# First two batches of a windowed attention: plain head pairs loaded in 1.5 KB runs and turned by fp32 products with the identity

## The chip, the cores and the metric

The kernel runs on one core of a Trainium2 chip. The metric is the device time of one execution in microseconds, the median of the runs of a kernel. The core has a matrix engine (TensorE, in the profile PE, its weight loads PEld), a vector engine (VectorE, DVE), a scalar engine (ScalarE, ACT), GpSimd (POOL), and SyncE (SP), which here issues all DMAs.

## The reference

Three layers follow each other; all inputs are float32.

```python
batch, n_heads, seq, head_dim = (4, 8, 576, 64)
scores = scale * np.matmul(q, k.transpose(0, 1, 3, 2))
mask_plain = (rel >= 0) & (rel < 32)
mask_dil = (rel >= 0) & (rel < 128) & (rel % 4 == 0)
masks = np.stack([mask_plain if h < H // 2 else mask_dil for h in range(H)], axis=0)
...                                     # softmax over the masked scores
x = (attn @ v), as [2304, 512]
h = x @ w_in                            # 512 -> 2048
x2 = (h - np.tanh(h)) @ w_out           # 2048 -> 512
...                                     # soft mixture of 8 experts of 4 slots each over x2
```

So each query of heads 0 to 3 (the plain heads) sees itself and the 31 keys before it, and each query of heads 4 to 7 (dilated) every fourth of the 128 last ones.

## The kernel before

Heads are taken in pairs: pairs 0 and 1 are plain, 2 and 3 dilated. For each of four batches the order is `PO = (2, 3, 0, 1)`. Batches 0 and 1 are laid out by a list of steps with due times (`at(t, f, ...)` and the loop that sorts them, from L778 on): scores, norms, transposes and values of batch 0, then of batch 1, between them the conversion of w_out and w_in and the first 512 tokens of the x @ w_in layer. Batches 2 and 3 run inside the loop over the hidden layer of batches 1 and 2 (class `Attn`), where TensorE multiplies without a break. The order of each engine's queue is the order in which the program is written.

The pieces that the change and the prediction speak of:

- `load_qk` (L206) brings q and k of one head pair into a tile `rqk` of 96 partitions. A partition x holds the rows 6x to 6x+5 of both heads. For plain pairs L214 interleaves the heads (row, head, 64 numbers), one DMA for each head and each of q and k, 256 bytes at a time. For dilated pairs L219 takes 3 KB runs, one DMA each for q and k. SP issues all of them in the order of the program and can wait only in that order.
- `emit_qk` (L247) turns one of q or k so that the head's 64 numbers lie in partitions: six TensorE transposes (L267) of 96 x 128 for a head pair, three into each of two PSUM tiles, each then copied out by ScalarE or VectorE (L97 for k, L275 or L277 for q, which is scaled on the way). The upper 64 partitions hold the second head.
- `emit_scores` (L283): mask product L291, scores L305 (for plain pairs 12 products of 64 x 64 weights and 96 moving columns, head 0 in the array's upper, head 1 in its lower rows), largest value L314 on VectorE, exponentials L317 on ScalarE.
- `emit_norm` (L323): 1/sum on VectorE (L326, L328), the product L329 on GpSimd. `emit_trans` (L332): transposes of the probabilities L338 on TensorE. `emit_pv` (L343): products with v, L359, one head into the lower, one into the upper half of the output's partitions.
- The w_out weights come as 64-bit numbers (`load_w`, L409) in tiles of 1 MB for two steps each; a step's conversion starts on GpSimd (L430), goes on on VectorE (L441 to L446) and feeds TensorE's transposes L468 and the products L479 and L492. Its float32 form is written back to HBM (L475).
- `emit_h` (L498): the products of the hidden layer, L503 to L505.

In the order by due time the loads of batch 0 stand among the w_out tiles: SP issues w_out steps 0 and 1 (4.53 us), v and then q and k of the first plain pair, w_out steps 2 and 3 (13.10 us), v of that pair, w_out steps 4 and 5, a write of w_out, q and k of the second plain pair, and so on.

Of the kernel before, what the change touches and what calls it, by code (L numbers as in the profile page):

```python
# [59 lines left out]
def moe_kernel(ctx: ExitStack, tc: tile.TileContext, q, k, v, w_in, w_out, phi, w1, w2, out):  # L60
    nc = tc.nc
# [4 lines left out]
    NP = H // 2  # L66
# [11 lines left out]
    def mm(shape):  # L78
        return ps_m.tile(shape, F32, tag="mm", name="mm")
# [15 lines left out]
    def copy(eng, out, in_):  # L95

        (nc.scalar.copy if eng == "A" else nc.vector.tensor_copy)(out=out, in_=in_)  # L97
# [7 lines left out]
    def unit(name, shape, dt=F32):  # L105
        return sb.tile(shape, dt, tag="unit", bufs=UNITS, name=name)

    def cpart(*dims):
        o = moff[0]
        moff[0] += size(dims)  # L110
        return view(mem[:, o:o + size(dims)], dims)
# [35 lines left out]
    ident = cpart(128)  # L147
# [55 lines left out]
    raws, vt, qT, kT = {}, {}, {}, {}  # L203
    sc_p, sc_s, sc_pt, qks = {}, {}, {}, []

    def load_qk(b, p):  # L206


        t = unit("rqk", [96, 2, 12 * D])
        for n, src in enumerate((k, q)):  # L210
            src = src[b, 2 * p:2 * p + 2]
            if p < NP // 2:
                for hh in range(2):
                    nc.sync.dma_start(  # L214
                        out=t[:, n].rearrange("x (a h d) -> x a h d", a=6, h=2)[:, :, hh, :],
                        in_=src[hh].rearrange("(x a) d -> x a d", a=6),
                    )
            else:
                nc.sync.dma_start(out=t[:, n], in_=src.rearrange("h (x a) d -> (h x) (a d)", a=12))  # L219
        raws[b, p] = t  # L220
# [26 lines left out]
    def emit_qk(b, p, n):  # L247

        if n == 0:
            if not qks:  # L250
                t = sb.tile([128, 2, 2 * S], F32, tag="qk", name="qk")
                qks.append(Ring([t[:, 0], t[:, 1]]))

            qT[b, p] = qks[0].next()
            kT[b, p] = qT[b, p][:, S:2 * S]
        raw = raws[b, p][:, n].rearrange("x (j c) -> x j c", j=6)
        t = qT[b, p][:, 0:S] if n else kT[b, p]
        if p < NP // 2:

            t = t.rearrange("p (x e r) -> p e r x", e=2, r=3)  # L260
        else:

            t = t.rearrange("p (h r x e) -> p r e h x", h=2, r=2, e=3)
        for th in range(2):
            ps = mm([128, 3, 96])
            for r in range(3):
                nc.tensor.transpose(ps[:, r, :], raw[:, 3 * th + r if p < NP // 2 else 2 * r + th], ident[0:96, 0:96])  # L267
            dst = t[:, th]
            if p >= NP // 2:
                ps = ps.rearrange("p e (h x) -> p e h x", h=2)  # L270
            eng = ENGS["qk"][4 * min(b, 2) + 2 * n + th]
            if n == 0:
                copy(eng, dst, ps)
            elif eng == "A":
                nc.scalar.activation(out=dst, in_=ps, func=ACTF.Copy, scale=0.125)  # L275
            else:
                nc.vector.tensor_scalar(out=dst, in0=ps, scalar1=0.125, scalar2=None, op0=ALU.mult)  # L277
# [439 lines left out]
    class Attn:  # L717
# [5 lines left out]
        def load(self, nqk, nv):  # L723
            while self.nqk < min(nqk, NP) or self.nv < min(nv, NP):
                if self.nqk < min(nqk, NP):
                    load_qk(self.b, PO[self.nqk])
                    self.nqk += 1
                if self.nv < min(nv, NP):
                    load_v(self.b, PO[self.nv], nc.sync)
                    self.nv += 1  # L730

        def turn(self, s):

            for p, n in ([(s, 0), (s, 1)] if s < 3 else [(3, s - 3)] if s < 5 else []):
                emit_qk(self.b, PO[p], n)
                if n:
                    self.load(p + 3, p + 2)
            if 0 < s <= NU // 2:
                for i in (2 * s - 2, 2 * s - 1):
                    emit_trans(self.b, i)  # L740
# [32 lines left out]
    with tc.manual_schedule():  # L773
# [7 lines left out]
        for b, (t0, dt) in enumerate((ATT0, ATT1)):  # L781
            for i in range(NU):
                t = t0 + dt * i
                at(t, emit_scores, b, i)
                at(t + NORM[b] * dt, emit_norm, b, i)
                at(t + TRANS[b] * dt, emit_trans, b, i)
                at(t + PV[b] * dt, emit_pv, b, i)
                if b == 0 and i < NWARM:
                    at(t + WAT * dt, warm, WARM)
            for p in range(NP):  # L790
                for n in range(2):
                    at(t0 - 0.02 + 0.01 * n if p == 0 else t0 + dt * (3 * p - 3 + n + QK[b]), emit_qk, b, PO[p], n)
                at(t0 + dt * 3 * p - LQK[b], load_qk, b, PO[p])
                at(t0 + dt * 3 * p - LV[b], load_v, b, PO[p], nc.sync)
        at(DT0 + ATT0[1] * 5, consts2)
        for p in range(2):
            at(ATT1[0] + ATT1[1] * (12 + 3 * p) - LQK[1], load_qk, 2, PO[p])
        at(ATT1[0] + ATT1[1] * 12 - LV[1], load_v, 2, PO[0], nc.sync)
        at(TPHI, lambda: nc.sync.dma_start(out=phi_sb, in_=phi.rearrange("(k p) s -> p k s", p=128)))
        for e in range(NFT):  # L800
            t, dt = (WO1[0] + WO1[1] * e, WO1[1]) if e < KA else (WO2[0] + WO2[1] * (e - KA), WO2[1])
# [6 lines left out]
            t, dt = WI[0] + WI[1] * e, WI[1]  # L808
# [11 lines left out]
        for ft in range(NFT):  # L820
            t = HT[0] + HT[1] * ft
# [23 lines left out]
        for ch in range(1, 4):  # L845
            xh, xl = xhi[ch], xlo[ch]
            if ch == 3:
# [6 lines left out]
                t = unit("gr", [128, 3, 512])  # L854
# [4 lines left out]
            for s in range(NFT // 2):  # L859
                a, b = 2 * s, 2 * s + 1  # L860
# [40 lines left out]
        for s in range(NFT // 2):  # L901
            a = 2 * s
            ps = ps_h.tile([128, 512], F32, tag="h", name="h").rearrange("p (i t) -> p i t", i=2)
# [57 lines left out]
        for a, copy in enumerate((nc.scalar.copy, nc.vector.tensor_copy)):  # L961
            ps = mm([128, 2, 128])
# [7 lines left out]
        ps = mm([128, 512])  # L970
        for c in range(4):
            for fq in range(4):
                nc.tensor.matmul(
                    ps[32 * fq:32 * fq + 32, :], lhsT=tT[:, c, 32 * fq:32 * fq + 32], rhs=wo[fq][:, c, :],
                    start=(c == 0), stop=(c == 3), tile_position=(0, 32 * fq),
# [7 lines left out]
        for a, copy in enumerate((nc.scalar.copy, nc.vector.tensor_copy)):  # L983
            ps = mm([128, 2, 32])
# [32 lines left out]
        for cols in halves:  # L1017
            ps = mm([96, 256])
# [3 lines left out]
                out=sS[64:96, cols], in0=ps[64:96], in1=sS[64:96, cols].bitcast(F32), op=ALU.subtract  # L1022
# [49 lines left out]
```

## Time and profile before

| | |
|---|---|
| median of 3 runs | 500.41 us (499.46 to 501.45) |
| the profiled execution | 501.07 us, its span 499.3 us |
| mean granted TensorE clock in it | 0.96 of full speed |
| busy in the span: PE, PEld | 470.8 us (94%), 351.4 us (70%) |
| DVE, ACT, POOL | 222.9, 236.0, 83.6 us |
| DMA packets | 60740, of them under 512 bytes 35600 |

The profile comes from one execution. It is read by stretch: TensorE is the busy engine nearly all the time, but not from the start. For the first 80 us the attention of batch 0, the conversion of the weights and the loads run against each other, and the granted clock of TensorE changes between its full and its half speed; later TensorE hardly pauses. A busy time of TensorE says that matmuls were under way, not how full the array was: matmuls overlap, and their time from start to end is longer than the time until the next one starts.

### The profile page before, as it was taken

To read this page: it belongs to the slowest core of one execution; us is meant where nothing else is said; L and a number is where in the kernel's file an instruction comes from. 1 tells how busy PE (TensorE), PEld (TensorE's weight loads), DVE (VectorE), ACT (ScalarE), POOL (GpSimd) and SP (SyncE) were. 2 spreads that over 40 slices of the span, in tenths; PEclk is the share of its full clock that TensorE was granted. 3 is DMA by queue.
4 is the path that set the end of the run, shared out by engine and by line. 5 is a ranking of instruction groups with operands and counts; after the bars stand their busy time and mean duration, and the time that the engine had idled before them with its cause. 6 is when DMAs were issued, how large, how long until landed. Compare 5 with 4: busy or idle time off the path is not lost.

```text
span 499.3 us, 11253 instructions
## 1 busy us (share of the span) xinstructions
PE 470.8 (94%) x4531; PEld 351.4 (70%) x4531; DVE 222.9 (45%) x558; ACT 236.0 (47%) x763; POOL 83.6 (17%) x99
## 2 busy tenths in 40 slices
PE   6989888999999999999999899999999999999981
PEld 4767676877777867888787678877678869845430
DVE  1787888954754445543252454332221223232132
ACT  3857536575655464665365356543132323313121
POOL 3463444432341010111011011100000000010000
PEclk9967768999999999999999999999999999999996
DMA  9997799444145401222320100209600259899938
GB/s 247 277 262 258 258 336 269 151 117 121 35 139 123 96 3 39 76 59 49 81 44 1 37 1 2 86 4 390 254 29 0 85 180 402 304 389 410 409 146 334
DMA packets 60740, 81.14 MB, mean 163 GB/s; under 512 B 35600, under 2 KB 39440, under 8 KB 60688
## 3 DMA queue, kind: packets, MB, share of 16 engines
q1 hardware_dynamic: 60688, 80.42, 49.7%
q8 instruction: 36, 0.59, 0.5%
q14 instruction: 16, 0.13, 0.1%
HBM read 71.50 MB, written 8.91 MB: 161 GB/s over the span
## 4 chain that ended last, share of the span: by engine, by line
PE 85%; DVE 6%; ACT 4%; issue 1%; DMA 1%; POOL 0%; POOLq 0%; ACTq 0%; DVEq 0%
PE h L503 14%; PE h L505 13%; PE h L504 13%; PE mm L305 6%; PE mm L537 5%; PE lg L518 4%; PE mm L359 4%; PE mm L338 4%; PE mm L635 3%; PE mm L267 3%; PE h L686 3%; PE y L711 3%; ACT mem L317 2%; PE warm L200 1%; PE mm L468 1%; PE mm L479 1%
## 5 line engine op out<-in xcount | busy, mean ns | idle before, releaser
L503 PE MATMUL h<-xhi,whi 128*128 128x512 f32 x256 | 107.1, 418 | 0.0
L505 PE MATMUL h<-xhi,wlo 128*128 128x512 f32 x256 | 101.0, 395 | 0.0
L504 PE MATMUL h<-xlo,whi 128*128 128x512 f32 x256 | 100.8, 394 | 0.0
L509 ACT ACTIVATE mem<-h 128x512 f32<-128x512 f32 x56 | 33.4, 596 | 83.7 <-PE h L505 83.7
L512 DVE TENSOR_TENSOR mem<-h,mem 128x512 f32<-128x512 f32 x56 | 38.6, 689 | 73.6 <-ACT mem L509 73.4
L329 POOL TENSOR_TENSOR mem<-mem 128x320 f32<-128x320 f32 (+1 forms) x48 | 34.5, 718 | 195.7 <-DVE mem L328 132.7
L503 PEld LDWEIGHTS h<-xhi,whi 128*128 128x128 f32 x256 | 48.8, 191 | 13.3 <-issue 5.0
L505 PEld LDWEIGHTS h<-xhi,wlo 128*128 128x128 f32 x256 | 48.5, 189 | 10.9
L504 PEld LDWEIGHTS h<-xlo,whi 128*128 128x128 f32 x256 | 48.9, 191 | 8.4
L97 ACT COPY g<-mm 128x512 f32<-128x512 f32 x72 | 40.2, 596 | 12.0 <-PE mm L550 4.8
L317 ACT ACTIVATE mem<-mm,mem 128x80 f32<-128x80 f32 (+1 forms) x84 | 26.8, 330 | 30.1 <-DVE mem L314 30.1
L305 PE MATMUL mm<-qk 64*64 64x96 f32 (+2 forms) x672 | 36.0, 254 | 2.1 <-DVE qk L97 2.0
L317 ACT ACTIVATE mem<-mem 128x80 f32<-128x80 f32 (+1 forms) x84 | 29.9, 357 | 16.5 <-DVE mem L314 14.5
L305 PEld LDWEIGHTS mm<-qk 64*64 64x64 f32 (+1 forms) x672 | 29.0, 139 | 10.6 <-issue 5.6
L97 ACT COPY mem<-mm 80x448 f32<-80x448 f32 (+4 forms) x64 | 26.7, 442 | 10.1 <-DVE xlo L391 6.5
L338 PE MATMUL mm<-mem 112*80 112x112 f32 (+1 forms) x168 | 25.4, 279 | 5.0 <-POOL mem L329 2.8
L311 DVE TENSOR_TENSOR mem<-mm,mem 128x320 f32<-128x320 f32 (+1 forms) x24 | 11.3, 470 | 41.8 <-PE mm L305 41.8
L512 DVE TENSOR_TENSOR gr<-h,gr 128x512 f32<-128x512 f32 x16 | 11.1, 691 | 42.2 <-ACT gr L509 42.2
L359 PEld LDWEIGHTS mm<-mem,v 80*64 80x64 f32 (+1 forms) x672 | 23.8, 144 | 7.8 <-issue 4.2
L359 PE MATMUL mm<-mem,v 80*64 80x48 f32 (+1 forms) x672 | 28.6, 234 | 0.0
L267 PE MATMUL mm<-mem,rqk 96*128 96x96 f32 x192 | 23.2, 262 | 5.1 <-DMA rqk<-in_k_dram 4.1
L460 POOL TENSOR_TENSOR wlo<-cvb,whi 128x512 fp32r<-128x512 f32 x16 | 21.5, 1343 | 38.0 <-DVE whi L97 14.4
(153 smaller groups left out, 749.3 us busy)
## 6 DMA issues: line engine op xcount, KB each, us to landing
ex<-in_moe_w_dram SPq DMA_DIRECT2D x30, 1024.0 KB, 10.6
raww<-in_moe_w_out_dram SPq DMA_DIRECT2D x8, 1024.0 KB, 8.7
raww<-in_moe_w_in_dram SPq DMA_DIRECT2D x8, 1024.0 KB, 5.9
wo_dram<-cva SPq DMA_DIRECT2D x16, 256.0 KB, 5.1
wo<-wo_dram SPq DMA_DIRECT2D x4, 1024.0 KB, 5.8
out_dram<-o SPq DMA_DIRECT2D x8, 512.0 KB, 4.8
v<-in_v_dram SPq DMA_DIRECT2D x24, 160.0 KB, 3.9
v<-in_v_dram SPq DMA_DIRECT2D x16, 192.0 KB, 3.4
```

Source lines behind the costliest of these rows:

```text
L97: (nc.scalar.copy if eng == "A" else nc.vector.tensor_copy)(out=out, in_=in_)
L267: nc.tensor.transpose(ps[:, r, :], raw[:, 3 * th + r if p < NP // 2 else 2 * r + th], ident[0:96, 0:96])
L305: nc.tensor.matmul(ps[64 * x:64 * x + nr, c, :], lhsT=qT[b, p][r, q0:q0 + nr], rhs=kT[b, p][r, k0:k0 + nk], start=not by_pe, stop=True, sk ...
L317: nc.scalar.activation(out=pr[:, c, :], in_=ps[:, c, :], func=ACTF.Exp, bias=nm[:, c:c + 1], accum_out=sm[:, c:c + 1],)
L329: nc.gpsimd.tensor_tensor(out=pr, in0=pr, in1=rc.unsqueeze(2).to_broadcast([128, nb, nk]), op=ALU.mult)
L338: nc.tensor.transpose(ps[:, c, :], pr[0:P, c, :], ident[0:P, 0:P])
L359: nc.tensor.matmul(o[64 * hh:64 * hh + 64, col:col + nq], lhsT=vt[b, p](n, hh), rhs=pt[:, c, 64 * x:64 * x + nq], start=True, stop=True,)
L503: nc.tensor.matmul(ps, lhsT=wh, rhs=xh[:, kt, :], start=(kt == 0), stop=False)
L504: nc.tensor.matmul(ps, lhsT=wh, rhs=xl[:, kt, :], start=False, stop=False)
L505: nc.tensor.matmul(ps, lhsT=wl, rhs=xh[:, kt, :], start=False, stop=(kt == KT - 1))
L509: nc.scalar.activation(out=g, in_=ps, func=ACTF.Tanh)
L512: nc.vector.tensor_tensor(out=g, in0=ps, in1=g, op=ALU.subtract)
```

## The change

For plain pairs of batches 0 and 1, `load_qk` issues one DMA for k and one for q instead of two each. Both heads' rows go one head behind the other into the partition, 6 rows x 64 numbers = 1.5 KB in one run. A transpose of 128 columns that are two heads' 64 can't be taken from that layout with one step, so `emit_qk` takes, for each of the six rows, two ordinary fp32 products: the head's 96 x 64 piece is the weight, the identity the moving operand (96 columns), and the result goes to the lower or the upper 64 partitions of the PSUM tile. What lies in PSUM, and all that follows, is the same. Batches 2 and 3 and the dilated pairs stay as they were.

```diff
--- before.py
+++ after.py
@@ -209,12 +209,16 @@
         t = unit("rqk", [96, 2, 12 * D])
         for n, src in enumerate((k, q)):
             src = src[b, 2 * p:2 * p + 2]
-            if p < NP // 2:
+            if p < NP // 2 and b >= 2:
                 for hh in range(2):
                     nc.sync.dma_start(
                         out=t[:, n].rearrange("x (a h d) -> x a h d", a=6, h=2)[:, :, hh, :],
                         in_=src[hh].rearrange("(x a) d -> x a d", a=6),
                     )
+            elif p < NP // 2:
+                nc.sync.dma_start(
+                    out=t[:, n].rearrange("x (h c) -> x h c", h=2), in_=src.rearrange("h (x a) d -> x h (a d)", a=6)
+                )
             else:
                 nc.sync.dma_start(out=t[:, n], in_=src.rearrange("h (x a) d -> (h x) (a d)", a=12))
         raws[b, p] = t
@@ -264,6 +268,14 @@
         for th in range(2):
             ps = mm([128, 3, 96])
             for r in range(3):
+                if p < NP // 2 and b < 2:
+
+                    for hh in range(2):
+                        nc.tensor.matmul(
+                            ps[64 * hh:64 * hh + 64, r, :], lhsT=raws[b, p][:, n, 64 * (6 * hh + 3 * th + r):][:, 0:64],
+                            rhs=ident[0:96, 0:96], start=True, stop=True,
+                        )
+                    continue
                 nc.tensor.transpose(ps[:, r, :], raw[:, 3 * th + r if p < NP // 2 else 2 * r + th], ident[0:96, 0:96])
             dst = t[:, th]
             if p >= NP // 2:
```

## Rows read from the trace of the kernel before

**Rows 1.** The page's granted TensorE clock, tenths of full speed, 40 slices of 12.5 us.
```profile
PEclk9967768999999999999999999999999999999996
```
**Rows 2.** By stretch: length, busy us of each engine (instructions), granted clock, DMA share, GB/s.
```profile
core 0: us, PE busy (x) PEld busy (x) DVE busy (x) ACT busy (x) POOL busy (x), PEclk, DMA share, GB/s
...
25.64:29.06 3.42, 2.10 (x36) 1.60 (x34) 2.00 (x7) 2.48 (x13) 3.20 (x6) 1.00 0.93 172
29.06:42.71 13.65, 13.59 (x120) 9.86 (x120) 10.71 (x25) 7.55 (x23) 6.42 (x8) 0.50 0.97 308
...
56.37:70.02 13.65, 11.49 (x69) 9.06 (x70) 11.47 (x25) 5.00 (x14) 7.69 (x6) 0.50 0.96 278
...
73.43:76.84 3.41, 1.64 (x17) 1.31 (x15) 3.35 (x5) 2.79 (x6) 2.91 (x2) 1.00 1.04 361
76.84:80.26 3.42, 3.23 (x37) 2.65 (x38) 1.96 (x5) 1.36 (x9) 0.00 (x0) 0.50 1.07 305
80.26:489.80 409.54, 402.14 (x3837) 299.11 (x3836) 167.45 (x432) 190.10 (x599) 47.37 (x52) 1.00 0.41 137
288.47:291.88 3.41, 2.66 (x25) 2.25 (x24) 2.39 (x10) 2.21 (x7) 0.72 (x1) 1.00 0.00 0
```
**Rows 3.** Waits, 22 to 31 us: total us, times, longest.
```profile
POOL cva L430 <- DMA raww<-in_moe_w_out_dram: 3.0, 1, 3.0
...
PE mm L338 <- POOL mem L329: 1.8, 2, 1.4
```
**Rows 4.** GpSimd in order of time: start us, us, operation, [idle before <-releaser].
```profile
22.08 1.05 POOL L430 TENSOR_TENSOR cva<-raww,mem 128x512 f32<-128x512 f32 x1 [3.03 <-DMA raww<-in_moe_w_out_dram]
...
27.34 1.04 POOL L430 TENSOR_TENSOR cva<-raww,mem 128x512 f32<-128x512 f32 x1
28.34 0.72 POOL L329 TENSOR_TENSOR mem<-mem 128x320 f32<-128x320 f32 x1
```
**Rows 5.** TensorE in order of time, around 29 us.
```profile
29.12 0.97 PE L338 MATMUL mm<-mem 112*80 112x112 f32 x4 [1.38 <-POOL mem L329]
...
30.36 1.22 PE L305 MATMUL mm<-qk 64*64 64x96 f32 x12
```
**Rows 6.** SP's issues in order of time: start us, us, line, xcount.
```profile
7.17 1.95 SPq L214 DMA_DIRECT2D rqk<-in_k_dram  x2
9.44 3.62 SPq L214 DMA_DIRECT2D rqk<-in_q_dram  x2
13.10 1.24 SPq L409 DMA_DIRECT2D raww<-in_moe_w_out_dram  x1
```
**Rows 7.** DMA packets from 12.4 to 14.4, 14.4 to 17.5 and 69.4 to 71 us.
```profile
DMA packets 1100, 0.43 MB, mean 213 GB/s; under 512 B 895, under 2 KB 1100, under 8 KB 1100
...
DMA packets 1590, 0.73 MB, mean 237 GB/s; under 512 B 1505, under 2 KB 1505, under 8 KB 1589
...
DMA packets 324, 0.63 MB, mean 396 GB/s; under 512 B 19, under 2 KB 19, under 8 KB 324
```
**Rows 8.** Tile rqk, 7 to 13 us: time from issue to landing.
```profile
DMA to landing us min/median/max: 7.3/7.4/8.1
```
**Rows 9.** ScalarE in order of time, around 29 us.
```profile
28.35 1.25 ACT L275 ACTIVATE qk<-mm 128x288 f32<-128x288 f32 x2
```
**Rows 10.** The chain that ended last, in order of time: start us, us, what.
```profile
38.10 1.15 PE mm L267 x6
...
41.10 1.15 PE mm L305 x12
...
46.11 0.64 PE mm L305 x12
...
47.11 0.50 PE mm L359 x12
...
112.39 0.50 PE mm L267 x6
```
**Rows 11.** TensorE by line and form, 288.47 to 291.88 us: busy us, mean ns.
```profile
L338 PE MATMUL mm<-mem 112*80 112x112 f32 x8 | 1.1, 261 | 0.7 <-ACT g L97 0.7
L537 PE MATMUL mm<-mem 128*128 128x128 f32 x8 | 1.0, 272 | 0.0
```

## The prediction

> **What bounds the kernel now.** I read the granted clock and the engines' shares by stretch first, because the edit lies in the first quarter of the span only. From 80 us on TensorE is busy 402.1 of 409.5 us at full clock [rows 2]: there nothing is gained except by giving TensorE less to do, and what was gained before 80 us arrives at the end unchanged. Before 80 us it is otherwise. TensorE's clock stands at its lower level (1.2 instead of 2.4 GHz) for three stretches, 29.06 to 42.71, 56.37 to 70.02 and 76.84 to 80.26 [rows 2]; they are the dips in the page's clock line [rows 1]. Before the first fall the engine was busy only 2.10 of 3.42 us, before the third 1.64 of 3.41 [rows 2]. In the low stretch that starts at 29.06 TensorE works almost without a pause (13.59 of 13.65 us), VectorE for 10.71 [rows 2].
>
> So I asked what makes the pause before 29.06. The waits from 22 to 31 us name it: GpSimd waits 3.0 us for a w_out tile to land, and TensorE 1.8 us, in two waits, for GpSimd [rows 3]. On GpSimd, in order: the conversion at L430 starts at 22.08, when its tile has landed; then come a normalisation, a mask, the next L430 at 27.34 and the normalisation L329 at 28.34 [rows 4]. TensorE's transposes L338 wait 1.38 us for that one and start at 29.12; the scores L305 follow at 30.36 [rows 5]. GpSimd is busy 3.20 of the 3.42 us up to 29.06 [rows 2], so a tile that lands sooner moves this whole string. SP had issued the first plain pair's loads just ahead of that tile: four pieces from 7.17 on, the tile at 13.10 [rows 6].
>
> **The change, part by part.**
>
> *Loads.* For pairs 0 and 1 of batches 0 and 1, four DMAs of 256-byte runs (4 x 576) become two of 1.5 KB runs (2 x 192); the bytes stay at 4 x 144 KB = 0.59 MB. From 12.4 to 14.4 us, where 895 of 1100 packets are under 512 bytes, the DMA engines move 213 GB/s, from 14.4 to 17.5, where 1505 of 1590 are, 237; from 69.4 to 71 us, where nearly all are larger than 2 KB, 396 [rows 7]. The old load thus takes 0.59/213 = 2.8 us of full DMA time. No row has 1.5 KB runs by themselves. If they go no faster than the small ones, nothing is gained (0); if as fast as the large ones, 0.59/396 = 1.5 us, a gain of 1.3. In size 1.5 KB is nearer to the large ones, so I take 1.0 us (0 to 1.3) for all that is queued behind the first load.
>
> The Trainium skill, DMA: Bandwidth & Descriptors, Specifications, gives 512 bytes as the least transfer for full rate. By that rule 1.5 KB runs go at the large ones' rate and the gain is the upper bound, 1.3 us. The trace agrees as far as its 213 against 396 GB/s reach, but other sizes are mixed in.
>
> *SP.* Two issues fewer per pair. The old ones took 1.95 us for two and 3.62 for two [rows 6], the last of them held back, and landed 7.3 to 8.1 us after issue [rows 8]. SP is free earlier, but the DMA engines behind it are full at that time, so I count nothing beside the 1.0 us. Were they not full, the tile could start up to 13.10 - 9.44 = 3.7 us sooner; I keep that for the clock rival. The second load stands ahead of weights that GpSimd takes after they have landed, and the two of batch 1 land long before their transposes after 100 us: 0, hidden under TensorE's unbroken work. Without that cover they would be worth up to 1.3 us each.
>
> *From the tile to TensorE.* 1.0 us earlier at L430, which waited 3.03 [rows 4], moves L329 and L338 by 1.0, L338 to 28.1. What is late next is ScalarE: the scores at 30.36 need its copies of q, L275, two from 28.35 lasting 1.25 us, so until 29.60 [rows 9]. The scores then gain at most 30.36 - 29.60 = 0.76. I take 0.75 (0 if the tile comes no earlier; 1.3 if ScalarE moves too). It is a lead in low-clock work, worth half once the clock is up again at 42.71: **-0.4 us** (0 to -0.7).
>
> *TensorE.* 48 transposes (8 groups of 6, 96 moving columns) become 96 products (8 groups of 12, two heads side by side in the array's columns). No row has that form; two are near. The scores L305, 12 fp32 products of 96 moving columns in pairs that share the array by rows, take 0.64 us at full clock and 1.15 at the low one; the values L359, 12 products that share it by columns as the new ones do, but with 64 moving columns, 0.50 [rows 10]. An old group of 6 takes 0.50 at full clock and 1.15 at the low one [rows 10]. If the pairs overlap, a new group is 0.50 to 0.64; if they don't, 12 x (0.50/6 = 0.083) = 1.0. I take 0.64, the row with the same moving width: L359 at 0.50/12 = 0.042 each is half of a transpose, so column pairs do overlap. At the low clock that is 1.15 for 1.15. At 112.39, between full-array work, 0.50 becomes 0.64; the changes of tiling beside it may cost as much again: +0.2. Of the other seven four follow L359 and two precede it, in the same tiling; a change of tiling saved is worth at most 0.14 (the same 0.64 - 0.50), and half of it on three groups that nothing hides is -0.2. Those before 27 us lie beside GpSimd's string and count nothing; uncovered they are 0.14 each, either way. Copies out of PSUM stay. **0.0 us** (-0.4 to +0.5).
>
> *Sum.* **-0.4 us.** The profiled execution is 501.07 us, 1.8 of it around its span of 499.3, and lies 0.7 above the median of 500.41. That makes the span 498.9, such an execution 500.7, and the median **500.0**.
>
> **The rivals.**
>
> *The clock doesn't fall at 29.06.* The pause before it shrinks from 1.38 us to what ScalarE still causes, and L338 moves ahead of 29.06. A stretch busy 2.66 of 3.41 us (288.47 to 291.88) kept the full clock, one busy 2.10 of 3.42 lost it [rows 2]; with the pause down to some 0.8 us the stretch before 29.06 would be busy about 2.6 of 3.42. Then 13.6 us of TensorE's work no longer takes twice its time, but VectorE, busy 10.71 of those 13.65, lets at most 2.9 be gained: I take 2.4, and with the 0.4 it is **497.6** (-2 to -4, where the tile comes sooner still). Against it: VectorE then sets the pace, TensorE pauses again, and the fall may only come later.
>
> The Trainium skill, TensorE: Matmul & The Clock Gate, Part 4, says that transposes don't count as activity for the clock as other products do. By that, 12 transposes turned into 24 products before 27 us would by themselves make this rival likelier. The trace speaks against the rule: from 288.47 to 291.88 at least 16 of the 25 TensorE instructions were transposes [rows 11] and the clock stayed at 1.00 [rows 2]. So this case's chance rests on the pause alone.
>
> *A fall that lasts longer: slower than before.* The third low stretch lasted 3.42 us, the two before it 13.65 [rows 2]. It follows a pause in which VectorE keeps TensorE waiting (1.64 of 3.41 busy). If the work arrives so shifted that this fall lasts as long as the others, 10.2 us more, of a stretch in which TensorE hardly rests, run at half speed: +5.1, less 0.4, **505.1**. It decides once TensorE's work after 76.84 is thinner than its 3.23 of 3.42 us now. For it: nothing pins the pauses. Against it: the shift that I expect is below 1 us.
>
> *Column pairs don't overlap.* 1.0 instead of 0.64 a group, six groups that nothing hides, one of them at half clock: 7 x 0.36 = +2.5, less 0.4: **502.5**. L359 speaks against it.
>
> *The loads move nothing.* The tile is held by something else, or another wait ends at the same time: **500.4**.
>
> **How the numbers follow.** Forecast 0.46; clock stays up 0.32; longer fall 0.08; no overlap 0.04; nothing moves 0.10. About 0.5%, 2.5 us, is what a measurement of this kernel can tell from no change. Faster than 497.9: most of the second case, 0.26. Slower than 502.9: the longer fall, part of no overlap, some other fall of the clock, 0.11. The rest, 0.63, is the same. The range takes in the clock case down to -3.9, and upwards loads without gain, the dearer TensorE groups and 1 us of scatter (the runs before reach 1.0 above their median): 496.5 to 501.9. It leaves out the longer fall, no overlap and the clock case's tail, under 2 in 10. The likeliest case's own range is 499.2 to 501.0.
>
> **What would show it.** L430 at 21.1 instead of 22.08, its wait 2.0; L338 near 28.1; L305 near 29.6; groups of 12 at 0.64 in the chain; 4 x (2304 - 384) = 7680 fewer packets. The clock line tells the rivals apart: the dips in their places (forecast), the first gone or later (clock case), the last longer (slower). I am wrong if L430 starts no earlier, or if a group takes 1.0 us.

## The result, and the profile after

The change makes the kernel slower by 0.3 to 0.9 per cent in the median; the first and the third interval lie above 1, the second just takes in 1. Three sets of runs of the changed kernel, each beside runs of the kernel before on the same chip, gave

| | changed | before | ratio [95%] |
|---|---|---|---|
| first set | 504.06 us (501.54 to 506.74, 8 runs) | 500.29 us (8 runs) | 1.0085 [1.0061, 1.0109] |
| second set | 502.16 us (498.01 to 504.37, 12 runs) | 499.72 us (34 runs) | 1.0027 [0.9996, 1.0058] |
| third set | 503.67 us (500.03 to 506.73, 12 runs) | 499.70 us (17 runs) | 1.0076 [1.0045, 1.0106] |

The forecast was 500.0 us with a range up to 501.9; the first and the third median lie above it by about 2 us, the second by 0.3. The profiled execution of the first set took 502.19 us, with a span of 500.4 (before: 501.07 and 499.3). It is the second fastest of its eight runs, and its span is only 1.1 us longer, where the medians are 3.8 apart.

The page's clock line of the changed kernel answers to [rows 1]. The dip that stood in the third and fourth slices (near 29 us) is gone; a new one stands in slice 23, near 280 us.

```profile
PEclk9999878999999999999999899999999999999996
```

The stretches of the changed kernel, in the columns of [rows 2]: first the two that held the pause and the low clock before, then the two at the new dip.

```profile
25.64:29.06 3.42, 2.49 (x52) 1.99 (x44) 2.00 (x7) 2.02 (x12) 3.20 (x5) 1.00 1.06 327
29.06:42.71 13.65, 11.64 (x188) 8.67 (x188) 13.27 (x29) 9.06 (x35) 6.91 (x8) 1.00 0.91 266
...
276.28:279.70 3.42, 1.79 (x16) 1.45 (x17) 2.64 (x6) 1.36 (x2) 0.00 (x0) 0.99 0.65 131
279.70:283.11 3.41, 3.41 (x12) 2.74 (x10) 0.00 (x0) 1.06 (x2) 0.00 (x0) 0.51 0.00 0
```

From 29.06 to 42.71 TensorE now runs at full clock (188 instructions instead of 120; 42 of the difference are the products that stand there for transposes), and VectorE sets the pace: busy 13.27 of 13.65 us. From 279.70 to 283.11 it works without a pause at the lower level, which it did not do before.

GpSimd and TensorE of the changed kernel in order of time, in the columns of [rows 4] and [rows 5] (L442 is L430 of before, L341 is L329, L350 is L338, L317 is L305; L274 are the new products):

```profile
22.19 1.05 POOL L442 TENSOR_TENSOR cva<-raww,mem 128x512 f32<-128x512 f32 x1 [3.65 <-PE mm L274]
...
28.45 0.73 POOL L341 TENSOR_TENSOR mem<-mem 128x320 f32<-128x320 f32 x1
```
```profile
26.33 1.21 PE L274 MATMUL mm<-mem,rqk 96*64 96x96 f32 x24
...
29.24 0.58 PE L350 MATMUL mm<-mem 112*80 112x112 f32 x4 [1.11 <-ACT qk L287]
...
29.97 0.71 PE L317 MATMUL mm<-qk 64*64 64x96 f32 x12
```

The conversion of the w_out tile starts at 22.19 (before 22.08), its normalisation at 28.45 (28.34), the transposes at 29.24 (29.12): between these two profiles nothing there came earlier. The first row names a product of TensorE (L274) as what ended the wait of 3.65 us, but the tile landed at 22.12 (issued at 9.73, 12.4 us to landing), 0.07 us before the conversion. A group of new products stands in the trace as 24 instructions and lasts 1.21 us. The chain that ended last, from 100 to 136 us, has four of them; the same four places of the kernel before follow in the second fence.

```profile
102.37 1.14 PE mm L274 x24
...
110.57 1.14 PE mm L274 x24
...
126.92 1.14 PE mm L274 x24
...
133.39 1.14 PE mm L274 x24
```
```profile
104.73 0.65 PE mm L267 x6
...
127.93 0.64 PE mm L267 x6
134.06 0.64 PE mm L267 x6
```

(The fourth, 0.50 at 112.39, is in [rows 10].) Four times 1.14 is 4.56; 0.65 + 0.50 + 0.64 + 0.64 is 2.43. The chain is longer by 2.1 us at a place where TensorE never pauses (busy 36.00 us of the 36.00 from 100 to 136, in both kernels).

So the profile holds three sizes. To separate them I took, for each kernel, the start of the same TensorE instruction minus its start in the profiled execution of before, at six places. This table is worked out from the traces and carries most of what follows; negative is earlier.

| kernel | at 29.1 us | at 44.8 | at 99.4 | at 140.1 | at 270.4 | at 287.4 | low clock from (first 50 us) | near 280 us |
|---|---|---|---|---|---|---|---|---|
| changed, first | +0.12 | -2.34 | -2.36 | -0.28 | -0.26 | +1.33 | none | 279.7 |
| changed, second (e0) | +0.07 | -2.40 | -2.62 | -0.54 | -0.48 | +1.14 | none | 279.1 |
| changed, third (e12) | +0.07 | +0.75 | -0.24 | +1.83 | +1.82 | +3.43 | 32.2 | 281.4 |
| e1, loads | -0.05 | -0.38 | -1.23 | -1.23 | -1.19 | -1.19 | 31.3 | none |
| e2, products | +1.46 | -1.02 | -0.16 | +1.91 | +1.91 | +3.51 | none | 281.6 |
| e3, batch 0 | -0.41 | -2.86 | -2.00 | -2.00 | -1.97 | -1.98 | none | none |
| e10, batch 0 again | -1.17 | -3.62 | -6.23 | -6.22 | -6.21 | -4.83 | none | 272.6 |
| e11, batch 0, v later | -1.08 | -0.41 | -1.41 | -1.41 | -1.37 | -1.38 | 31.0 | none |
| e4, products of batch 0 | +0.11 | +0.45 | -1.31 | -1.31 | -1.25 | -1.27 | 31.3 | none |
| e7, batch 1 | +1.86 | -0.48 | -1.07 | +1.01 | +1.01 | +2.61 | 24.6 | 280.6 |
| e8, one pass | -0.95 | -3.41 | -3.87 | -4.87 | -4.81 | -3.31 | none | 274.3 |
| e5, earlier filler | +0.41 | 0.00 | -0.85 | -0.85 | -0.79 | -0.79 | 31.6 | none |
| e9, late filler | +1.06 | +1.05 | +0.44 | +2.37 | +2.42 | +3.99 | 26.5 | 282.5 |

In the changed kernel's first row: 2.46 us gained between 29 and 45 us, 2.08 lost between 99 and 140, 1.59 lost between 270 and 287. With -0.2 behind that, the sum at the end is +1.1.

### The profile page after: what moved, and what is told of

Read it like the earlier page. It is cut to its first block, busy times and chain, and to the rows that moved or that the text cites. A ratio compares the mean times of both kernels' runs of the same rounds, so it can differ in the third digit from the quotient of the medians.

```text
span 500.4 us, 11528 instructions
## 1 busy us (share of the span) xinstructions
PE 469.0 (94%) x4675; PEld 350.8 (70%) x4675; DVE 225.5 (45%) x558; ACT 235.7 (47%) x763; POOL 84.0 (17%) x99
## 2 busy tenths in 40 slices
DMA packets 52933, 81.16 MB, mean 162 GB/s; under 512 B 26256, under 2 KB 31632, under 8 KB 52880
## 4 chain that ended last, share of the span: by engine, by line
PE 81%; DVE 9%; ACT 4%; issue 2%; POOL 1%; DMA 1%; POOLq 0%; ACTq 0%; DVEq 0%
PE h L515 14%; PE h L517 13%; PE h L516 13%; PE mm L549 5%; PE mm L317 5%; PE lg L530 4%; PE mm L371 4%; PE mm L647 3%; PE mm L350 3%; PE h L698 3%; PE y L723 3%; PE mm L279 2%; ACT mem L329 2%; DVE cva L455 2%; PE warm L200 1%
## 5 line engine op out<-in xcount | busy, mean ns | idle before, releaser
L341 POOL TENSOR_TENSOR mem<-mem 128x320 f32<-128x320 f32 (+1 forms) x48 | 34.5, 719 | 195.5 <-DVE mem L340 135.6
L329 ACT ACTIVATE mem<-mm,mem 128x80 f32<-128x80 f32 (+1 forms) x84 | 26.9, 332 | 30.4 <-DVE mem L326 30.4
L329 ACT ACTIVATE mem<-mem 128x80 f32<-128x80 f32 (+1 forms) x84 | 29.9, 357 | 16.5 <-DVE mem L326 14.4
L317 PE MATMUL mm<-qk 64*64 64x96 f32 (+2 forms) x672 | 33.7, 244 | 2.1 <-DVE qk L97 1.9
L317 PEld LDWEIGHTS mm<-qk 64*64 64x64 f32 (+1 forms) x672 | 27.1, 131 | 10.1 <-issue 4.6
L350 PE MATMUL mm<-mem 112*80 112x112 f32 (+1 forms) x168 | 24.2, 269 | 6.6 <-POOL mem L341 2.9
L521 ACT ACTIVATE gr<-h 128x512 f32<-128x512 f32 x16 | 9.6, 600 | 38.3 <-PE h L517 38.3
```

The costliest lines, as they stand in the source:

```text
L317: nc.tensor.matmul(ps[64 * x:64 * x + nr, c, :], lhsT=qT[b, p][r, q0:q0 + nr], rhs=kT[b, p][r, k0:k0 + nk], start=not by_pe, stop=True, sk ...
L329: nc.scalar.activation(out=pr[:, c, :], in_=ps[:, c, :], func=ACTF.Exp, bias=nm[:, c:c + 1], accum_out=sm[:, c:c + 1],)
L341: nc.gpsimd.tensor_tensor(out=pr, in0=pr, in1=rc.unsqueeze(2).to_broadcast([128, nb, nk]), op=ALU.mult)
L350: nc.tensor.transpose(ps[:, c, :], pr[0:P, c, :], ident[0:P, 0:P])
L521: nc.scalar.activation(out=g, in_=ps, func=ACTF.Tanh)
```

## The experiments

The kernel before had medians of 499.7 to 500.3 us beside them.

**The changed kernel again (e0).** No edit.

> The changed kernel once more, unedited, for a second profile and more times. Theory 1 (the products cost it): every fp32 product stands in the trace as two instructions, a group of 12 products is 24 instructions and 1.0 us instead of 0.5, so the four groups after 100 us again lose about 2.0 us together in this profile, wherever the clock falls; time 503 to 505. Theory 2 (the clock): the low-clock stretches lie elsewhere in each execution, and the time follows them; a second profile with other falls then has another time, by 2 us or more, and the groups after 100 us lose little.

Measured: the second set above, 502.16 us, ratio 1.0027 [0.9996, 1.0058]; span 501.4. The three sizes come out again: -2.47, +2.08, +1.62. The groups are as theory 1 had them; the median lies below its 503 to 505.

**The loads alone (e1).** The new loads, but the branch with the products taken out, so that the old transposes take two rows of one head instead of one row of two heads: q and k are turned wrongly, the work is that of before.

```diff
-                if p < NP // 2 and b < 2:
-                    for hh in range(2):
-                        nc.tensor.matmul(
...
-                    continue
```

> The new loads alone: the 1.5 KB runs stay, the products are taken out and the six transposes of 128 neighbouring columns stand in their place. What is turned is then two rows of one head instead of one row of two heads, so the plain pairs of batches 0 and 1 are not computed as the reference has them; all instructions else, their sizes and their order are those of the kernel before. Theory 1: without the products nothing is lost after 100 us, and the earlier loads give 0 to 2 us: 498.5 to 500.5, against 500.3 before. Theory 2 (new loads shift the start of the work and with it the falls of the clock): as slow as the change, 502.5 to 505.

**The products alone (e2).** The old loads, and the products on their layout.

```diff
-            if p < NP // 2 and b >= 2:
+            if p < NP // 2:
...
-                            ps[64 * hh:64 * hh + 64, r, :], lhsT=raws[b, p][:, n, 64 * (6 * hh + 3 * th + r):][:, 0:64],
+                            ps[64 * hh:64 * hh + 64, r, :], lhsT=raw[:, 3 * th + r, 64 * hh:64 * hh + 64],
```

> The products alone: the loads stay as before (four DMAs of 256-byte runs, heads interleaved), only the six transposes become twelve products on the old layout. Theory 1: eight groups lose 0.5 us each, four of them after 100 us where nothing hides it: 502.5 to 504.5, at least 2.0 over the kernel before. Theory 2: 500 to 501, since the loads haven't moved. If products hold the clock up where transposes don't, the first low stretch near 29 us is absent here as well and the loss before 80 us is made good: 501 to 503.

Measured: e1 499.09 us, ratio 0.9986 [0.9960, 1.0013]; e2 503.10 us, 1.0068 [1.0044, 1.0091]. The loss comes with the products. What the loads do is seen in e1's trace: the DMA engines from 14.4 to 17.5 us, to be set against 237 GB/s of before in [rows 7], and the start of the conversion on GpSimd, in the columns of [rows 4].

```profile
DMA packets 403, 0.99 MB, mean 319 GB/s; under 512 B 32, under 2 KB 244, under 8 KB 402
```
```profile
22.03 1.04 POOL L434 TENSOR_TENSOR cva<-raww,mem 128x512 f32<-128x512 f32 x1 [3.50 <-DMA raww<-in_moe_w_out_dram]
```

The DMA engines do move more in that stretch, though not with 1.5 KB runs alone (about 160 of the 403 packets are over 2 KB), and the conversion starts at 22.03, only 0.05 us before the time in [rows 4]. But that one time was an early one. Over the profiles with the old loads in batch 0 (before, e2, e4, e5, e7, e9) the conversion starts at 22.08, 23.55, 22.19, 22.50, 23.21 and 23.15, on the mean at 22.78; over those with the new loads (three of the changed kernel, e1, e3, e8, e10) at 22.19, 22.16, 22.16, 22.03, 21.67, 21.14 and 20.91, on the mean at 21.75. In the table the same two groups stand at 29.1 us at +0.82 (before counted as 0) and at -0.33. So over these profiles the loads bring the tile about 1.0 us sooner and the transposes behind it about 1.1 (for the three profiles of the changed kernel alone 0.6 and 0.7), and in the time of the kernel by themselves 0.6 us, with an interval (0.9960 to 1.0013) that takes in zero.

**The change in batch 0 only (e3, and the same again as e10).**

```diff
-            if p < NP // 2 and b >= 2:
+            if p < NP // 2 and b >= 1:
...
-                if p < NP // 2 and b < 2:
+                if p < NP // 2 and b < 1:
```

> The whole change for batch 0 alone; batch 1 is loaded and turned as before. Theory 1: the four groups after 100 us are transposes again, and the 2.0 us lost there come back: 500 to 502.5, and if the gain before 80 us of the profiled execution of the change (2.3 us at 103 us) is the rule, below 499. Theory 2: as the change, 503 to 505, since everything that moves the falls of the clock before 80 us is still in.

> The whole change for batch 0 alone, once more, for a closer interval and a second profile. If the gain of the first look (0.3%, with an interval that just reaches no change) is real: 497.5 to 499, no fall of the clock near 279 us, and the pause near 276 us 195.6 to 195.8 us after the last rise. If it was scatter: 499.5 to 500.5.

Measured: e3 498.14 us, 0.9970 [0.9939, 1.0001]; e10 497.37 us (496.06 to 499.20), 0.9948 [0.9929, 0.9966]. e10's interval lies below 1, e3's just reaches it: this is the version that is faster than the kernel before and than the changed one. Between 99.4 and 140.1 us both stand still in the table (-2.00 to -2.00, -6.23 to -6.22): without products in batch 1 the 2.08 us are gone. e10's profiled execution missed my expectation in its low stretches: the one near 76 us is absent too, and one stands at 272.6. Its clock line:

```profile
PEclk9999889999999999999999899999999999999997
```

**The products of batch 0 alone (e4)**, on old loads: e2 with `b < 1` in place of `b < 2`.

> Products on the old loads, for batch 0 alone; batch 1 and all loads as before. Theory A (in batch 0 it is the products that gain, by keeping the clock up after 29 us; the loads give nothing): no low-clock stretch near 29 us, 2.8 us gained between 29 and 42 us in the profile, and the same time as the whole change for batch 0 alone, 497.5 to 499. Theory B (the new loads are what gains there): no better than before, 499.5 to 501.

Measured: 499.00 us, 0.9982 [0.9958, 1.0006]. Again nothing is lost after 99 us. But the low stretch of before is there (31.3 to 41.5): in this execution the products in batch 0 did not keep the clock up. In e2, which has the same loads and the same batch 0, the stretch is absent, so one profile of either does not settle it. The time lies at the upper edge of theory A, with the low stretch that theory B expects.

**The change in batch 1 only (e7).**

```diff
-            if p < NP // 2 and b >= 2:
+            if p < NP // 2 and b != 1:
...
-                if p < NP // 2 and b < 2:
+                if p < NP // 2 and b == 1:
```

> The whole change for batch 1 alone: batch 0 is loaded and turned as before, the four late groups are products. Theory 1: nothing before 100 us, 2.0 us lost in the four groups: 501.5 to 502; if the fall of the clock at 279 us, which the three profiles with products in batch 1 show and the three without don't, belongs to the shift by 2 us, 1.6 more: 503 to 503.6. Theory 2 (late groups are hidden): 499.5 to 500.5.

Measured: 503.57 us, 1.0087 [1.0056, 1.0118]. The two losses of the changed kernel (+2.08 and +1.60) without its gain.

**Products of one pass (e8).** The same 96 products, but of the upper halves of the numbers read as bf16; q and k of these pairs lose their lower 16 bits.

```diff
-                            ps[64 * hh:64 * hh + 64, r, :], lhsT=raws[b, p][:, n, 64 * (6 * hh + 3 * th + r):][:, 0:64],
-                            rhs=ident[0:96, 0:96], start=True, stop=True,
+                            ps[64 * hh:64 * hh + 64, r, :], lhsT=raws[b, p].bitcast(BF16)[:, n, 128 * (6 * hh + 3 * th + r) + 1:][:, 0:127:2],
+                            rhs=ident.bitcast(BF16)[0:96, 1:192:2], start=True, stop=True,
```

> The change with each product taken on the upper halves of the numbers (bf16 views of the same bytes), so that q and k of the plain pairs of batches 0 and 1 lose their lower 16 bits. Theory 1 (an fp32 product is two passes of the array and two instructions): a group has 12 instructions instead of 24 and takes 0.45 to 0.65 us instead of 1.0; of the 2.0 us lost in the four groups after 100 us at most 0.6 is left; 1.5 to 2 us faster than the change. Rival (the loss comes from the changes of tiling around the groups): as many us lost as in the change.

Measured: 499.22 us, 0.9979 [0.9955, 1.0002]. The new lines by their source, all eight groups together (instructions with shortest, median and longest ns, first and last start), first the changed kernel, then e8, then the first of e8's groups in its chain:

```profile
L274 PE MATMUL mm<-mem,rqk x192: 246/246/297, 21.5 to 134.3; 96*64 96x96 f32 x192
```
```profile
L274 PE MATMUL mm<-mem,rqk x96: 203/208/235, 22.1 to 129.8; 96*64 96x96 bf16 x96
...
100.86 0.39 PE mm L274 x12
```

The program writes 96 products. They stand as 192 instructions in fp32 and as 96 in bf16: an fp32 product is two instructions. In the changed kernel's trace the starts of one group lie 7 and 76 ns apart in turn, so that two column halves start together and each couple takes 0.083 us; 24 instructions are 12 couples, 12 x 0.083 = 1.0 us, and a couple of products, two such couples of instructions, 0.166. An old transpose is a single instruction, six of them start 0.083 apart, 0.5 us. In e8 the couples follow each other after some 0.045 us, and a group takes 0.39 in the chain, less than the 0.45 to 0.65 that were expected and less than the old transposes. So the column pairs overlap in both; what costs is the second instruction of each product and its length: the two instructions of a couple take not twice but nearly four times e8's one (0.166 against 0.045). Late in the span e8 gains 1.00 us (-3.87 to -4.87) where fp32 loses 2.08.

**A filler before batch 0's pause (e5).** `NWARM = 4` becomes 5: 1.24 us more of bf16 products on TensorE, no other edit of the kernel before. They are ten products, one instruction each; the expectation counts five.

> The kernel before with five more warm-up products (bf16, ten instructions, 1.24 us) at the fifth score step of batch 0, just ahead of the pause in which TensorE's clock falls at 29 us; loads and transposes as before. Theory A: work that fills the pause is enough, whoever does it: no low stretch near 29 us, and 1.5 to 2.9 us faster than before, 497 to 498.5. Rival: what counts is that the transposes are replaced; the fall comes as before, and the filler costs nothing or its 1.24 us: 499.7 to 501.

Measured: 500.03 us, 0.9992 [0.9968, 1.0016]. The low stretch came all the same, from 31.6 to 41.9. More work for TensorE ahead of the pause doesn't suffice. The filler did not fill the pause itself: it stands at 21.41, and in front of L338 TensorE still waits 1.38 us, as before. Theory A, work in the pause, was thus not tested.

**A late filler (e9).** The kernel before with 17 bf16 products of 256 columns at one place near 130 us, to delay what follows by as much as the four groups do, without any of the change.

```diff
+        def fill(n):
+            ps = mm([128, 256])
+            w = ident.bitcast(BF16)
+            for _ in range(n):
+                nc.tensor.matmul(ps, lhsT=w[:, 0:128], rhs=w, start=True, stop=True)
+        at(115.0, fill, 17)
```

> The kernel before with 17 bf16 products on the identity (about 2.0 us) put into TensorE's order once, behind a late group of transposes near 130 us; loads and transposes as before, no product of the change is in it. In ten profiles so far the pause of TensorE near 276 us starts 195.6 to 195.8 us after the clock's last rise near 80 us and no fall follows in the five kernels without products in batch 1, and 197.4 to 197.8 us (once, with short products, 194.8) in the five with them, and a fall near 279 us that costs 1.5 to 1.6 us follows. Theory 1 (the second loss comes from where the shift by 2 us puts that pause): a low stretch near 279 us here too, 2.0 + 1.6 us lost: 503 to 504. Rival (the products themselves bring the fall): 2.0 lost and no low stretch near 279: 501.5 to 502.3.

Measured: 504.06 us, 1.0084 [1.0061, 1.0108], as slow as the changed kernel. In its profiled execution the filler takes its time (first line, the chain), and then the clock falls after the pause near 280 us (second and third, stretches in the columns of [rows 2]).

```profile
129.02 1.86 PE mm L801 x17
```
```profile
276.00:282.50 6.50, 4.76 (x45) 2.39 (x37) 3.09 (x7) 1.45 (x3) 0.00 (x0) 1.00 0.33 69
282.50:285.91 3.41, 3.41 (x11) 2.73 (x9) 0.00 (x0) 0.91 (x2) 0.00 (x0) 0.50 0.00 0
```

+1.93 at the filler and +1.57 at the fall: without a single new product. The fall near 280 us thus comes with a delay of 2 us that no product of the change made. The profiled execution took 508.25 us, the longest of the six runs. A further 3.2 us were lost in it behind 465 us, where TensorE waits 0.34 and 1.37 us for loads of in_moe_w_dram and the clock is at its lower level from 487.28 on.

**Batch 0 with v's loads behind the tile (e11).** With the new loads SP issues the w_out tile at 9.4 to 9.7 us and v's small pieces right behind it, from 9.8 to 10.2, where before they came at 14.39 (the tile at 13.10, [rows 6]). e11 puts them later.

```diff
-LV = (4.31, 7.03)
+LV = (2.0, 7.03)
```

> The change for batch 0 alone, and the loads of v are due 2.3 steps later, which moves v of the first plain pair (256-byte runs) behind the w_out tile that GpSimd waits for near 22 us, and behind the next one. Theory (that tile lands no earlier with the new loads because v's small pieces are now issued right behind it and share the DMA engines with it): the tile's conversion starts at 20.0 to 21.2 instead of 21.7 to 22.2, the pause of TensorE near 28 us gets shorter by about as much, and the time is that of the change for batch 0 alone or up to 1.5 us less. Rival (the tile's own 1 MB and what stands before it take all the time): the conversion still starts at 21.7 to 22.2, and the time stays.

Measured: 497.74 us, 0.9963 [0.9938, 0.9989], as e3 and e10. The conversion on GpSimd:

```profile
21.00 1.04 POOL L442 TENSOR_TENSOR cva<-raww,mem 128x512 f32<-128x512 f32 x1 [2.33 <-DMA raww<-in_moe_w_out_dram]
```

It starts at 21.00, with v's loads now issued behind two tiles, at 17.93 us; but e10 without this edit had 20.91 and e3 21.67, and one profile each can't tell the edit from that. The time did not follow: with this early tile the first fall came nevertheless (31.0).

**The changed kernel a third time (e12).** No edit; it was run because the two medians before lay 1.9 us apart.

> The changed kernel a third time: its two medians (504.06 and 502.16 us) lie 1.9 us apart, and both profiles (spans 500.4 and 501.4) stand for executions without a low stretch near 29 us. Theory (three sizes make the time: -2.85 us where the fall near 29 us is missing, +2.0 for the four late groups of 24 instructions, +1.6 for the fall near 279 us): four L274 x24 groups of 1.14 to 1.21 us after 100 us; a low stretch of 3.4 us that starts between 279 and 285; the pause ahead of it 197.2 to 197.8 us after the last rise near 80; a span of 499.8 to 501.6 where there is no low stretch near 29 us, of 502.6 to 504.6 where there is one. Median 502 to 504. Rival (something not in this account costs the slower executions 2 us or more, a second fall near the end for example): a span above these bounds with the same low stretches, or a further low stretch after 300 us that is not the last one. A pause 197.2 to 197.8 us after the rise without a fall would refute the reading of the fall near 279.

Measured: the third set, 503.67 us; its profiled execution 504.40 us, span 502.6. Its clock line has both dips:

```profile
PEclk9978878999999999999999899999999999999997
```

The low stretch is back at 32.2, nothing is gained between 29 and 45 us (+0.68 instead of -2.46), and the losses of 2.07 and 1.61 stay. The span lies at the edge of what was written down for this case. Medians of 502.2 to 504.1 fit executions of which some have the first fall and some don't: +1.1 and +2.1 in the two profiles without it (e0's has 0.95 us from behind 466 us in it, where TensorE waits 0.92 us for a load of in_moe_w_dram), +3.3 in the one with it. That is not the whole spread. The three profiled executions had a mean granted clock of 0.974, 0.976 and 0.967; of the 32 runs of the changed kernel seven lie below 0.965, with a median of 506.0 us (504.4 to 506.7). These had the low clock for longer than any profile of the changed kernel shows, and where in the span stays open; e9's late low stretch is one place.

## Why the prediction was wrong

**TensorE: the step that failed.** I read "x12" beside the scores and the values in [rows 10] as 12 products, and the list of the kernel's pieces says 12 as well. The program issues six there, two heads by three blocks; the twelve are instructions, two to a product. So the row that I chose as the nearest, 0.64 us, was the price of six products, and twelve cost 2 x 0.50 plus the 0.14 that I had for a change of tiling, 1.14, which is just what each new group takes in the chain. The term that I put at 0.0 us (-0.4 to +0.5) is +2.1: four groups at 1.14 for 2.43 us of old ones. A count against the code, 672 instructions of L305 against the 336 products that its loops issue, would have shown it before.

The Trainium skill, FP8 and Floating Point Precision, TensorE Precision Notes, says that a true fp32 product makes four passes through the array. The trace agrees in size: a couple of products in two column halves takes 2 x 0.083 = 0.166 us in fp32, about four times the 0.045 of e8's couple in one pass. By it, from e8's 0.045, six couples are 6 x 4 x 0.045 = 1.1 us, an estimate, against 1.0 measured.

**The rival "column pairs don't overlap"** had the right price, 1.0 us a group, by the wrong mechanism. The halves start 7 ns apart in the trace, and e8 keeps that order at 0.39 us a group. Its sum was too high in one point (six groups counted where nothing hides them) and lacked the fall near 280 us. The four groups after 100 us cost their full price. Those ahead of it cost little: where the low clock stands after 31 us, the profiles with products in batch 0 (e4, e11, e12) lose 0.3 to 0.7 us between 29.1 and 44.8, those without (e1, e5) gain 0.3 to 0.4, and by 99.4 us the two can't be told apart (-0.2 to -1.4 and -0.9 to -1.2).

**The loads.** This step held in the mean of many profiles. With 1.5 KB runs the DMA engines moved 276 GB/s in the changed kernel (first line below) and 319 in e1 from 14.4 to 17.5 us, between the 237 and the 396 of [rows 7], and there are 60740 - 52933 = 7807 packets fewer (I had 7680). The tile's conversion came 1.0 us sooner on the mean of six and seven profiles, where I had 1.0; the transposes L338 about 1.1, where I had 1.0. As the starts spread over 1.3 to 1.5 us in either group, the agreement to the tenth is luck in part. The 0.6 us of e1's median stand beside my -0.4, with an interval that takes in zero. What didn't hold are the single numbers that I had named as its test, 21.1 at L430 and 28.1 at L338: they were reckoned from one profile of before, whose 22.08 lies at the early end of the 22.08 to 23.55 that the same loads give. By my own test ("wrong if L430 starts no earlier") I'd have thrown out a step that the means bear out. SP's order changed as well (second fence, the columns of [rows 6]): the tile is issued 3.4 us sooner and v's small pieces right behind it. It then lands 12.4 us after its issue, where it was 8.9 before; whether v's pieces are the reason, e11 could not tell.

```profile
DMA packets 413, 0.85 MB, mean 276 GB/s; under 512 B 32, under 2 KB 308, under 8 KB 413
```
```profile
9.73 0.39 SPq L421 DMA_DIRECT2D raww<-in_moe_w_out_dram  x1
10.16 0.47 SPq L232 DMA_DIRECT2D v<-in_v_dram  x1
...
12.71 3.79 SPq L238 DMA_DIRECT2D v<-in_v_dram  x2
```

Whether ScalarE is what L338 waits for next stays open. The changed kernel's row names it (1.11 us, L287), but GpSimd's normalisation ends at 28.45 + 0.73 = 29.18 too, 0.06 us before the transposes start, as the one of before does (29.06 and 29.12).

**The clock at 29 us.** I gave this rival 0.32 and a gain of 2.4 us. It was right in size: 2.45 to 2.48 between 29.1 and 44.8 us in all six profiles in which the first fall is absent and the work the same, and VectorE, busy 13.27 of 13.65 us, leaves little more to gain there. By my signs the clock line (the first dip gone) named this rival, and the time lay above my range even so, for the products and the fall near 280 us cost 3.7. The fall near 29 us was missing in six of nine profiles with products in batch 0, and in none of five without them. My condition for it, that the tile comes sooner, was not what decided: in the three profiles of the changed kernel the conversion starts at 22.16 to 22.19, twice without the fall and once with it, and with it at 21.00 in e11. Nor did the length of the pause in front of the transposes: 1.11 and 1.10 us without the fall, 0.99 (e12) and 0.49 (e11) with it.

The Trainium skill, TensorE: Matmul & The Clock Gate, Part 4, says that transposes don't count as activity for the clock in the way that other products do. I had set it aside on account of [rows 11]. Six of nine against none of five is on its side; that three profiles with products (e4, e11, e12) show the fall, between 31.0 and 32.2, is not, and the products are also simply longer, 2.49 busy us instead of 2.10 up to 29.06. Against that stands e8, whose groups are shorter than the transposes (0.39 against 0.50 us) and whose one profile has no fall. No run here separates the two.

What does differ between two executions of the same kernel is when the clock first rises. In the changed kernel it rose at 10.00 and 9.40 us in the profiles without the fall and at 11.74 in the one with it; in the kernels of batch 0 alone at 10.12 and 9.79 without, at 10.51 (e11) and 10.79 (e4) with it. The waits are the same: at 32 us TensorE waits 1.05 us for VectorE in the first and in the third profile of the changed kernel. The reading at hand is that the same pause makes the clock fall or not by how long after the rise it comes. Of the nine profiles with products in batch 0 two don't fit it as it stands: in e2 and e8, whose work stands 1.4 us later and 1.0 earlier at 29.1 us, the clock rose at 11.93 and 11.52, without a fall. It was read from the traces and not tested.

**A fall that I had no place for.** My slower rival was a longer third stretch; it stayed at 3.41 us in all profiles that have it. The fall came elsewhere, at a pause that I hadn't looked at. TensorE of the changed kernel, in the columns of [rows 5]; then the same place before:

```profile
275.68 1.30 PE L279 MATMUL mm<-mem,rqk 96*128 96x96 f32 x9
277.76 0.47 PE L279 MATMUL mm<-mem,rqk 96*128 96x96 f32 x3 [0.78 <-ACT qk L287]
279.08 1.15 PE L350 MATMUL mm<-mem 112*80 112x112 f32 x8 [0.85 <-ACT qk L287]
```
```profile
275.94 1.30 PE L267 MATMUL mm<-mem,rqk 96*128 96x96 f32 x9
278.02 0.47 PE L267 MATMUL mm<-mem,rqk 96*128 96x96 f32 x3 [0.77 <-ACT qk L275]
279.36 0.84 PE L338 MATMUL mm<-mem 112*80 112x112 f32 x7 [0.87 <-ACT qk L275]
```

The second view ends at 280 us, so that its last row counts seven of eight instructions. The waits are alike (0.78 and 0.85 against 0.77 and 0.87). The place is not. From the clock's last rise to the first of these lines it is 275.94 - 80.26 = 195.7 us before and 275.68 - 78.27 = 197.4 in the changed kernel. Over all profiles in which the last rise stands between 76 and 82 us:

| from the last rise to the pause's first line | kernels | clock falls after it |
|---|---|---|
| 194.8 us | e8 | yes, at 274.3 |
| 195.6 to 195.8 us | before, e1, e3, e4, e5, e11 | no |
| 197.3 to 197.8 us | changed (three profiles), e2, e7, e9 | yes |

What the products add after 100 us moves the pause by 2 us against the rise, and so does e9's filler, and the same pause then costs 1.5 to 1.6 us more. e10, whose last rise is at 64.41, has the fall too, 205.3 us after it. That it takes no product of the change is shown by e9. That the place decides fits all 14 profiles and was not tested apart from the delay; which places are safe is known for these distances only.

**The sum.** The -0.4 us of my forecast were, in the changed kernel's first profile, -2.46 (clock near 29 us), +2.08 (four groups), +1.59 (fall near 280 us) and about -0.1 of other shifts: +1.1. In the third profile +0.7 took the place of the first term, with -1.0 between 45 and 99 us: +3.3. The first set's median, 3.8 above the kernel before, is nearer to the third profile than to the first.

## What to carry to other kernels

Before pricing an instruction by a row, count the row against the code: the profile counts what the engine executes, and an fp32 product is two of it where an fp32 transpose is one. A saving or a cost in a stretch that has cover (here batch 0) and the same edit in a stretch that has none (here batch 1) are two edits; made apart, one is worth 0.3 to 0.5%, the other costs 0.9%. Where a kernel has short pauses near which the clock holds, a delay of 2 us ahead of them can cost nearly as much again (here 1.6 us); and a start read from one profile of before is one draw, here from a spread of 1.5 us.

## What was not expected of the hardware

- A couple of fp32 products of 96 x 64 weights and 96 moving columns, in the two column halves, takes 0.166 us (four instructions); one fp32 transpose of 96 x 128 takes 0.083; a couple in bf16 0.045.
- A pause with equal waits is followed by a low clock in some executions and not in others, of the same kernel too, and the clock's first rise moves between 9.40 and 11.99 us from one execution to the next.
- 1.5 KB runs moved 276 and 319 GB/s in mixed traffic, and a 1 MB tile issued 3.4 us sooner (9.73 instead of 13.10) started its conversion on the mean only 1.0 us sooner.
